# A cached decode block on one core: VectorE's part written as a loop, a head group's output steps placed in the next group's scores, load buffers at multiples of 512 bytes

## The chip, the cores and the metric

The kernel runs on one core of a Trainium2 chip. The core has five engines that work at the same time, each on its own list of instructions: TensorE (PE; its weight loads are listed as PEld), VectorE (DVE), ScalarE (ACT), GpSimd (POOL) and SyncE (SP), which here issues nearly all loads. The loads themselves are carried out by 16 DMA engines. Engines wait for each other through semaphores. The metric is the device time of one execution in microseconds (us); lower is better.

## The reference

One token for each of two sequences goes through grouped-query attention over a cache of 32768 keys and values and, beside it, through a small two-layer network; the two results are multiplied and added to the input. Everything is bf16.

```python
B, Sq, D = 2, 1, 512
Hq, Hkv, Sk, Dh = 32, 8, 32768, 128          # k_cache, v_cache: (B, Hkv, Sk, Dh)
xn = layernorm(A_x)
q = (xn @ wq) as (B, Hq, 1, Dh)              # four query heads share one cache head
scores = einsum("bhqd,bhkd->bhqk", q, k) * Dh ** -0.5
o = einsum("bhqk,bhkd->bhqd", softmax(scores), v)
s = o.reshape(B, Sq, Hq * Dh) @ wo           # wo: (4096, 512)
h2 = gelu(layernorm(xn) @ w3) @ w4           # with S = 1 the shifted branch through w1, w2 gives zero
g = silu(xn + h2)
return A_x + s * g
```

The two caches are 268 MB of the 280.5 MB that are read. Each of their bytes is used once, for four query heads.

## The kernel before

**Tiling.** The 16 pairs of a sequence and a cache head are the head groups (`groups`, L171). A group has 8 MB of keys and 8 MB of values. A group's rows are laid over 128 partitions, 64 KB to each, and its 32768 keys are cut into two halves of 128 keys a partition (`NPART` = 2, `SLOT` = 32 KB a partition). Keys go to `kbuf`, which has three slots of a half; a group uses slots 0 and 1 or 1 and 2 by turns. Values go to `vbuf`, two slots, reused by every group.

**One group, in order.** VectorE transposes the keys of a half in eight steps into four small buffers `T0` to `T3` (L383), 16 steps a group. TensorE multiplies each by the query (L432, four matmuls a step) and sums the eight steps of a half in one PSUM bank, `sc[0]` or `sc[1]`. VectorE takes the largest score of each half (`peak`, L373 and L374), TensorE spreads it (L438), VectorE makes the shift (L390, L391), ScalarE the exponentials (L392), VectorE their transposes (L397). TensorE sums the weights (L443) and multiplies them by the values (L451, 64 matmuls into `o`). Then come the group's **output steps**: ScalarE copies `o` to `ob` (L402); TensorE turns it (`oT`, L460); VectorE divides by the sum (`on`, L403 and L404); TensorE spreads the result (`xp`, L466); VectorE keeps the right quarter of it and stores it in the group's column of `oX` (L405, L408). After the last group TensorE multiplies `oX` by `wo` (L479, 128 small matmuls, 16 for each cache head); VectorE multiplies by `g4` and adds the input (L412, L413); two small stores write the output (L415).

**What sets the order.** Every engine's list is written out by hand. `Queue.op` (L47) puts the wait for the last event it needs on the instruction itself. TensorE's part of the 16 groups is a loop of 16 turns (`nc.Fori`, L423) that counts semaphores down (`take`, L419); VectorE's, ScalarE's and SyncE's parts are written out for all 16 groups. In each engine's list the output steps of a group stand between its values and the next group's keys: VectorE starts the transposes of group m+1 only after L408 of group m.

**The loads.** SyncE issues them in the order wq, w3, w4, keys of group 0, values of group 0, keys of 1, values of 1 and so on, each key or value load as one transfer of 8 MB. The keys of group m wait until the first half of the scores of group m-1 is done (`half`, L334: that frees slot 1, the only slot that two groups in a row share). The values of group m wait until the values of group m-1 have been multiplied (L346). The last group's keys and values come as two transfers each, a half at a time (L342, L330). Behind them, three transfers bring `wo` into slot 0 of `kbuf` (L348: four, three and one of the eight cache heads). L474 makes the products of cache head k wait for its own column of `oX` and its own part of `wo`.

**Where the buffers lie.** The tiles are placed one behind another in the order of L114 to L161, `kbuf` first.

Of the kernel before, what the change touches and what calls it, by code (L numbers as in the profile page):

```python
# [13 lines left out]
PE = mybir.EngineType.PE  # L14

KPT = 128
RT = 16
VT = 4
# [46 lines left out]
def kernel(  # L65
# [32 lines left out]
    SLOT = KPT * Dh  # L98
    NQ = 4
# [8 lines left out]
    def sb(name, shape, dt):  # L108
        return pool.tile(shape, dt, name=name)
# [3 lines left out]

    kbuf = sb("kbuf", [128, 3 * SLOT], BF16)  # L114
# [45 lines left out]
    g = sb("g", [B, D], F32)  # L160
    oX = sb("oX", [128, Hkv, NQ, B], BF16)  # L161

# [12 lines left out]
    def sem(name):  # L175
        return tc.alloc_semaphore(name)
# [12 lines left out]
    d_k = [sem(f"d_k{i}") for i in range(2)]  # L189
    d_wo = [sem(f"d_wo{i}") for i in range(len(wo_parts))]  # L190
    t_T, t_z, t_mx, t_pt, t_ob, t_on = (sem(f"t_{n}") for n in ("T", "z", "mx", "pt", "ob", "on"))
    t_v = [sem(f"t_v{i}") for i in range(NPART)]
    s_T, s_X = sem("s_T"), sem("s_X")
# [9 lines left out]
    NX = 5  # L203

    def order(m):
        return (1, 0) if m % 2 == 0 else (0, 1)

    with tc.tile_critical(no_gpsimd_drain=True):
# [4 lines left out]
        sp.op(lambda e: e.dma_start(out=kbuf[:, 0:NPART * SLOT], in_=row_view(A_k_cache, *groups[0])), inc=(d_k[0], 16))  # L213
# [119 lines left out]
        for m in range(1, NG):  # L333
            half = (s_T, NT * (m - 1) + NR)  # L334
            base = m % 2
            if m < NG - 1:
                sp.op(lambda e, m=m, base=base: e.dma_start(
                    out=kbuf[:, base * SLOT:(base + NPART) * SLOT], in_=row_view(A_k_cache, *groups[m])),
                    half, e_q, inc=(d_k[0], 16))
            else:  # L340
                for h in range(NPART):
                    sp.op(lambda e, m=m, h=h, base=base: e.dma_start(  # L342
                        out=kbuf[:, (base + h) * SLOT:(base + h + 1) * SLOT],
                        in_=row_view(A_k_cache, *groups[m])[:, h * SLOT:(h + 1) * SLOT]),
                        half, inc=(d_k[h], 16))
            load_v(m, (s_X, NX * (m - 1) + 3))  # L346
        for i, (a, c) in enumerate(wo_parts):
            sp.op(lambda e, a=a, c=c: e.dma_start(out=wo3[:, a:c, :], in_=wos[:, a:c, :]), (s_T, NT * (NG - 1)), inc=(d_wo[i], 16))  # L348


        e_oX = [None] * NG
        for m in range(NG):
            b, k = groups[m]
            first, second = order(m)

            def put_z(b, k):
                for j in range(4):
                    c = (NR - 1) * rep + 32 * j
                    ac.op(lambda v, j=j, c=c: v.copy(  # L359
                        out=z[32 * j:32 * j + 32, :, :, c:c + rep],  # L360
                        in_=qr[32 * j:32 * j + 32, :, :, b, k * rep:(k + 1) * rep]),
                        e_qr, e_z0, inc=(t_z, 1) if j == 3 else False)

            if m == 0:
                put_z(b, k)

            def landed(h):
                if m < NG - 1:
                    return (d_k[0], 16 * (m + 1))
                return (d_k[h], 16 * NG if h == 0 else 16)  # L370

            def peak(i):
                e = ve.op(lambda v: v.tensor_reduce(out=mx[:, i:i + 1], in_=sc[i][:, :], axis=AX.X, op=ALU.max), (s_T, m * NT + (i + 1) * NR))  # L373
                ve.op(lambda v: v.tensor_scalar_mul(out=mxr[:, i, :], in0=row_of[:, :], scalar1=mx[:, i:i + 1]), e,  # L374
                      inc=(t_mx, 1) if i == NPART - 1 else False)

            for i, h in enumerate((first, second)):
                u = m % 2 + h
                kt = kbuf[:, u * SLOT:(u + 1) * SLOT].bitcast(I32)
                for r in range(NR):  # L380
                    n = m * NT + i * NR + r
                    used = (s_T, n - T_BUFS + 1) if n >= T_BUFS else None
                    ve.op(lambda v, n=n, r=r, kt=kt: v.transpose(  # L383
                        out=Ts[n % T_BUFS][:, :].rearrange("p (b t k) -> p t b k", b=NB, t=RT),
                        in_=kt[:, r * W:(r + 1) * W].rearrange("p (t b k) -> p t b k", b=NB, t=RT)),
                        landed(h), used, inc=(t_T, 1))
                    if i == 1 and r == 3:
                        peak(0)
            peak(1)
            e = ve.op(lambda v: v.tensor_reduce(out=top[:, :], in_=S[:, rep:], axis=AX.X, op=ALU.max), (s_X, NX * m + 1))  # L390
            e = ve.op(lambda v: v.tensor_scalar_mul(out=shift[:, :], in0=top[:, :], scalar1=-inv_sqrt_dh), e)  # L391
            e_exp = [ac.op(lambda v, i=i: v.activation(  # L392
                out=ep[i][:, :], in_=sc[i][:, :], func=ACT.Exp, scale=inv_sqrt_dh, bias=shift[:, :], accum_out=rs[i][:, :]),
                e, e_tf if m == 0 else None) for i in range(NPART)]
            for i, h in enumerate((first, second)):
                ve.op(lambda v, i=i: v.tensor_scalar_mul(out=sm[i][:, :], in0=sel_h[:, :], scalar1=rs[i][:, 0:1]), e_exp[i], e_selh, inc=False)  # L396
                ve.op(lambda v, i=i, h=h: v.transpose(  # L397
                    out=pt[h][:, :, :].rearrange("p r (t h) -> p t r h", h=rep),
                    in_=ep[i][:, :].rearrange("p (t r h) -> p t r h", r=NR, h=rep)), inc=(t_pt, 1))
            if m < NG - 1:  # L400
                put_z(*groups[m + 1])
            ac.op(lambda v: v.copy(out=ob[:, :], in_=o[:, :]), (s_X, NX * m + 3), inc=(t_ob, 1))  # L402
            e = ve.op(lambda v: v.reciprocal(out=rec[:, :], in_=S[:, 0:rep]), (s_X, NX * m + 2))  # L403
            ve.op(lambda v: v.tensor_mul(out=on[:, :], in0=oT[:, :], in1=rec[:, :]), e, (s_X, NX * m + 4), inc=(t_on, 1))  # L404
            e = ve.op(lambda v: v.tensor_mul(  # L405
                out=xm[:, :, :], in0=xp_b[:, :].rearrange("p (r h) -> p r h", r=NQ), in1=mask[:, :, :]), (s_X, NX * m + 5))
            with nc.allow_low_precision(reason="three of the four terms are zero, the fourth is bf16"):
                e_oX[m] = ve.op(lambda v: v.tensor_reduce(out=oX[:, k, :, b], in_=xm[:, :, :], axis=AX.X, op=ALU.add), e)  # L408
# [10 lines left out]
        def take(s, n=1):  # L419
            nc.tensor.wait_ge(s, n).then_inc(s, -n)  # L420

        pe.wait(e_o0, e_ones, e_const, e_hf, e_tf)
        with nc.Fori(0, NG, engines=[PE], head_slot={PE: 0}):  # L423
            take(t_z)
            for i in range(NPART):
                for r in range(NR):
                    take(t_T)
# [10 lines left out]
            nc.tensor.matmul(  # L438
                S[:, rep:], lhsT=same_h[:, :], rhs=mxr[:, :, :].rearrange("p i r -> p (i r)"),
                start=True, stop=True).then_inc(s_X, 1)  # L440
            take(t_pt, NPART)
            for i in range(NPART):
                ins = nc.tensor.matmul(S[:, 0:rep], lhsT=ones_f[:, :], rhs=sm[i][:, :], start=(i == 0), stop=(i == NPART - 1))  # L443
            ins.then_inc(s_X, 1)
            for h in range(NPART):
                take(t_v[h], 16)
# [10 lines left out]
            ins.then_inc(s_X, 1)  # L457
            take(t_ob)
            for t in range(VT):
                ins = nc.tensor.matmul(  # L460
                    oT[:, :], lhsT=ob[:, t * Dh:(t + 1) * Dh], rhs=sel_o[:, t, :],
                    start=(t == 0), stop=(t == VT - 1))
            ins.then_inc(s_X, 1)
            take(t_on)
            for r in range(NQ):
                ins = nc.tensor.matmul(  # L466
                    xp_b[:, r * rep:(r + 1) * rep], lhsT=sel_r[:, r, :, :].rearrange("p j w -> p (j w)"), rhs=on[:, :],
                    start=True, stop=True)
            ins.then_inc(s_X, 1)
# [43 lines left out]
```

## Time and profile before

| | |
|---|---|
| median of three runs | 662.71 us (662.61 to 662.96) |
| the profiled execution, its own time | 663.0 us |
| span of the profiled execution, first to last instruction | 661.0 us |
| mean granted TensorE clock | 0.812 of full speed |
| busy share of PE, DVE, ACT | 64%, 56%, 8% |
| read from HBM | 280.50 MB, 424 GB/s over the span |

The profile describes one execution. "Busy" counts the time in which an engine's unit works; an engine can be half idle and still set the end, if something late waits for it. A row of DMA queues gives the packets of a queue, their megabytes, and the time that all its packets took as a share of the span times 16 DMA engines. In the timeline a row holds a start, a duration, the engine, the line of the kernel, what is written and from what, and how many instructions are merged (x64); in brackets stands how long the engine had been idle and what ended that. A "landing" is the time from the issue of a transfer to the completion of all its 16 shares.

### The profile page before, as it was taken

The numbers are of one execution on the slowest core, as the hardware profiler recorded it, in microseconds if no ns is written. First come the engines' busy times: TensorE is split into PE (matmuls) and PEld (weight loads), VectorE is DVE, ScalarE is ACT, GpSimd is POOL, SyncE is SP. The second block draws the span as 40 slices with busy tenths as digits, with TensorE's granted clock in tenths as the row PEclk, the third lists the DMA queues.
The fourth block names the chain that finished last, engine by engine and source line by source line (L and its number), as shares of the span: only waits on it lengthen the run. The fifth ranks groups of instructions, "written<-read, shape, count | busy, mean of one in ns | idle before, by whom it ended". The sixth has DMA issues, their size and how long they took to land. (4 is left out here: it accounts for less than half of the span.)

```text
span 661.0 us, 6555 instructions
## 1 busy us (share of the span) xinstructions
PE 422.7 (64%) x2642; PEld 176.3 (27%) x2674; DVE 373.2 (56%) x526; ACT 50.0 (8%) x152; POOL 1.7 (0%) x10
## 2 busy tenths in 40 slices
PE   2537586665758656485865648576565947656775
PEld 2312233222223322232332213222222322222323
DVE  4248192764819376381936629194672928558481
ACT  1110101010010101001010100101010010101000
POOL 1000000000000000000000000000000000000000
PEclk9959687787968769796877979788696976869798
DMA  8999999999999999999999999999999999999994
GB/s 363 444 430 440 437 444 436 409 437 436 440 440 433 420 428 436 444 440 432 412 436 436 445 436 432 412 440 436 444 436 432 412 437 436 444 432 409 424 413 183
DMA packets 6461, 280.61 MB, mean 425 GB/s; under 512 B 682, under 2 KB 692, under 8 KB 1716
## 3 DMA queue, kind: packets, MB, share of 16 engines
q1 hardware_dynamic: 6408, 280.50, 98.4%
q8 instruction: 4, 0.07, 0.0%
q14 instruction: 5, 0.04, 0.0%
q10 hardware_dynamic: 44, 0.01, 0.0%
HBM read 280.50 MB, written 0.00 MB: 424 GB/s over the span
## 5 line engine op out<-in xcount | busy, mean ns | idle before, releaser
L432 PE MATMUL sc<-T,z 128*128 128x512 bf16 x992 | 275.1, 422 | 133.9 <-PEq L420 127.9
L383 DVE STREAM_TRANSPOSE T<-kbuf 128x1024 int32<-128x1024 int32 x256 | 292.1, 1208 | 76.3 <-DMA kbuf<-in_A_k_cache_dram 76.3
L432 PEld LDWEIGHTS sc<-T,z 128*128 128x128 bf16 x1024 | 97.8, 103 | 304.9 <-issue 227.4
L451 PE MATMUL o<-vbuf,pt 128*16 128x512 bf16 x1024 | 92.8, 542 | 0.0
L404 DVE TENSOR_TENSOR on<-oT,rec 128x4 bf16<-128x4 f32 x16 | 2.6, 162 | 117.8 <-PE oT L460 117.8
L392 ACT ACTIVATE ep<-sc,shift 128x512 bf16<-128x512 f32 x32 | 21.7, 683 | 461.2 <-DVE shift L391 461.2
L451 PEld LDWEIGHTS o<-vbuf,pt 128*16 128x16 bf16 x1024 | 31.0, 119 | 54.0 <-issue 47.4
L443 PE MATMUL S<-sm,ones_f 128*128 128x4 f32 x64 | 14.6, 333 | 48.2 <-PEq L420 48.2
L373 DVE TENSOR_REDUCE mx<-sc 128x1 f32<-128x512 f32 x32 | 21.5, 671 | 20.0 <-PE sc L432 20.0
L443 PEld LDWEIGHTS S<-sm,ones_f 128*128 128x128 f32 x64 | 13.6, 298 | 49.9 <-issue 49.9
L460 PE MATMUL oT<-sel_o,ob 128*128 128x4 f32 x128 | 16.4, 252 | 12.6 <-PEq L420 12.6
L397 DVE STREAM_TRANSPOSE pt<-ep 128x512 bf16<-128x512 bf16 x32 | 22.6, 705 | 0.0
L460 PEld LDWEIGHTS oT<-sel_o,ob 128*128 128x128 f32 x128 | 15.5, 191 | 20.2 <-issue 20.2
L438 PE MATMUL S<-mxr,same_h 128*128 128x64 f32 x32 | 6.5, 285 | 18.4 <-PEq L420 18.4
L402 ACT COPY ob<-o 128x512 f32<-128x512 f32 x16 | 9.4, 586 | 113.7 <-PE o L451 113.7
L396 DVE TENSOR_SCALAR sm<-sel_h,rs 128x4 f32<-128x4 f32 x32 | 6.7, 209 | 13.6 <-ACT ep L392 13.6
L359 ACT COPY z<-qr 32x16 bf16<-32x16 bf16 x64 | 12.6, 197 | 3.9 <-issue 3.3
L403 DVE RECIPROCAL rec<-S 128x4 f32<-128x4 f32 x16 | 2.9, 183 | 17.5 <-PE S L443 17.5
L438 PEld LDWEIGHTS S<-mxr,same_h 128*128 128x128 f32 x32 | 4.8, 188 | 26.2 <-issue 26.2
L390 DVE TENSOR_REDUCE top<-S 128x1 f32<-128x64 f32 x16 | 3.6, 225 | 9.4 <-PE S L438 9.4
L374 DVE TENSOR_SCALAR mxr<-row_of,mx 128x32 f32<-128x32 f32 x32 | 7.7, 242 | 1.1
L466 PE MATMUL xp<-on,sel_r 128*128 128x4 bf16 x64 | 3.8, 164 | 5.5 <-PEq L420 5.5
(70 smaller groups left out, 64.2 us busy)
## 6 DMA issues: line engine op xcount, KB each, us to landing
kbuf<-in_A_k_cache_dram SPq DMA_DIRECT2D x2, 4096.0 KB, 22.7
vbuf<-in_A_v_cache_dram SPq DMA_DIRECT2D x2, 4096.0 KB, 21.7
kbuf<-in_A_wq_dram SPq DMA_DIRECT2D x1, 4096.0 KB, 12.4
vbuf<-in_B_w_dram SPq DMA_DIRECT2D x2, 1792.0 KB, 18.9
kbuf<-in_A_wo_dram SPq DMA_DIRECT2D x1, 2048.0 KB, 31.1
kbuf<-in_A_wo_dram SPq DMA_DIRECT2D x1, 1536.0 KB, 34.3
kbuf<-in_A_wo_dram SPq DMA_DIRECT2D x1, 512.0 KB, 34.9
kbuf<-in_A_k_cache_dram SPq DMA_DIRECT2D x15, 28.1
```

What stands on the lines that cost most here:

```text
L359: ac.op(lambda v, j=j, c=c: v.copy(out=z[32 * j:32 * j + 32, :, :, c:c + rep], in_=qr[32 * j:32 * j + 32, :, :, b, k * rep:(k + 1) * rep]) ...
L373: e = ve.op(lambda v: v.tensor_reduce(out=mx[:, i:i + 1], in_=sc[i][:, :], axis=AX.X, op=ALU.max), (s_T, m * NT + (i + 1) * NR))
L374: ve.op(lambda v: v.tensor_scalar_mul(out=mxr[:, i, :], in0=row_of[:, :], scalar1=mx[:, i:i + 1]), e, inc=(t_mx, 1) if i == NPART - 1 else ...
L383: ve.op(lambda v, n=n, r=r, kt=kt: v.transpose(out=Ts[n % T_BUFS][:, :].rearrange("p (b t k) -> p t b k", b=NB, t=RT), in_=kt[:, r * W:(r ...
L392: e_exp = [ac.op(lambda v, i=i: v.activation(out=ep[i][:, :], in_=sc[i][:, :], func=ACT.Exp, scale=inv_sqrt_dh, bias=shift[:, :], accum_ou ...
L397: ve.op(lambda v, i=i, h=h: v.transpose(out=pt[h][:, :, :].rearrange("p r (t h) -> p t r h", h=rep), in_=ep[i][:, :].rearrange("p (t r h) ...
L402: ac.op(lambda v: v.copy(out=ob[:, :], in_=o[:, :]), (s_X, NX * m + 3), inc=(t_ob, 1))
L432: ins = nc.tensor.matmul(sc[i][:, :], lhsT=z[:, nb, w, zc:zc + 128], rhs=Tb[:, nb, :, w], start=(r == 0 and nb == 0 and w == 0), stop=(r = ...
L438: nc.tensor.matmul(S[:, rep:], lhsT=same_h[:, :], rhs=mxr[:, :, :].rearrange("p i r -> p (i r)"), start=True, stop=True).then_inc(s_X, 1)
L443: ins = nc.tensor.matmul(S[:, 0:rep], lhsT=ones_f[:, :], rhs=sm[i][:, :], start=(i == 0), stop=(i == NPART - 1))
L451: ins = nc.tensor.matmul(o[32 * j:32 * j + VT * rep, :], lhsT=pt[h][:, r, a * VT * rep:(a + 1) * VT * rep], rhs=vt[:, u * VT:(u + 1) * VT, ...
L460: ins = nc.tensor.matmul(oT[:, :], lhsT=ob[:, t * Dh:(t + 1) * Dh], rhs=sel_o[:, t, :], start=(t == 0), stop=(t == VT - 1))
```

## The change

Six things are changed.

1. **VectorE's part of the head groups is a loop** of eight turns with two groups a turn (two, because a group's slots of `kbuf` alternate). The waits are no longer on the instructions: each is an instruction of its own in front of the one that needs it (`take`), which also counts the semaphore down. There are new semaphores for this: `t_used` for a `T` buffer that may be overwritten, `t_k[i]` for the i-th half of the keys that is worked on, `t_top`, `t_S`, `t_e`, `t_d`, `t_oT`, `t_xp`.
2. **The output steps of group m stand in the scores of group m+1.** TensorE turns `ob` between the two halves of the scores (`head_oT`) and spreads `on` after the fourth step of the second half (`head_xp`). VectorE divides after `peak(0)` (`head_on`) and keeps the quarter after the last transpose (`head_out`). The first group does these steps on zeros (`ob` is set to zero at the start); after the loops they are done once more for the last group.
3. **`oX` is written by ScalarE.** In a loop VectorE cannot name the group's column, so it writes to `oXs`, and ScalarE, whose part is still written out, copies that into the column (`keep_oX`), ahead of the next exponentials. All products with `wo` now wait for the last of these copies.
4. **The keys of the next group are issued** when the first matmul of `head_oT` behind the first half of the scores is done (`s_half`) in place of when the first half is done.
5. **`wo` is issued** behind the values of group 14 (`s_pv`), as the last values are, where it waited for the last scores of group 14 before; it stood behind the last values in SyncE's list before, and still does.
6. **An unused tile `lead`** of 384 bytes a partition ahead of `kbuf` puts `kbuf` and `vbuf` at multiples of 512 bytes; the tiles began at byte 16512 of a partition (`SB0`).

```diff
+    SB0 = 16512
+    sb("lead", [128, (-SB0) % 512 // 2], BF16)
     kbuf = sb("kbuf", [128, 3 * SLOT], BF16)
...
+    oXs = sb("oXs", [128, NQ], BF16)
...
+        po.op(lambda e: e.memset(ob[:, :], 0.0), inc=(t_ob, 1))
...
-            half = (s_T, NT * (m - 1) + NR)
...
-                    half, e_q, inc=(d_k[0], 16))
+                    (s_half, m), e_q, inc=(t_k[0], 16))
+                nc.sync.sem_inc(t_k[1], 16)
...
-            load_v(m, (s_X, NX * (m - 1) + 3))
+            load_v(m, (s_pv, m))
...
-            sp.op(lambda e, a=a, c=c: e.dma_start(out=wo3[:, a:c, :], in_=wos[:, a:c, :]), (s_T, NT * (NG - 1)), inc=(d_wo[i], 16))
+            sp.op(lambda e, a=a, c=c: e.dma_start(out=wo3[:, a:c, :], in_=wos[:, a:c, :]), (s_pv, NG - 1), inc=(d_wo[i], 16))
...
+        def keep_oX(m):
+            b, k = groups[m]
+            return ac.op(lambda v: v.copy(out=oX[:, k, :, b], in_=oXs[:, :]), (s_oX, m + 2))
...
         for m in range(NG):
+            if m:
+                keep_oX(m - 1)
+            for i in range(NPART):
+                ac.op(lambda v, i=i: v.activation(
+                    out=ep[i][:, :], in_=sc[i][:, :], func=ACT.Exp, scale=inv_sqrt_dh, bias=shift[:, :], accum_out=rs[i][:, :]),
+                    (s_shift, m + 1), e_tf if m == 0 else None, inc=(t_e, 1))
...
+        e_oX = keep_oX(NG - 1)
...
+        def head_on():
+            take(nc.vector, t_oT, 2)
+            nc.vector.tensor_mul(out=on[:, :], in0=oT[:, :], in1=rec[:, :]).then_inc(t_on, 1)
+
+        def head_out():
+            take(nc.vector, t_xp)
+            nc.vector.tensor_mul(
+                out=xm[:, :, :], in0=xp_b[:, :].rearrange("p (r h) -> p r h", r=NQ), in1=mask[:, :, :]).then_inc(t_d, 1)
+            take(nc.vector, t_d)
             with nc.allow_low_precision(reason="three of the four terms are zero, the fourth is bf16"):
-                e_oX[m] = ve.op(lambda v: v.tensor_reduce(out=oX[:, k, :, b], in_=xm[:, :, :], axis=AX.X, op=ALU.add), e)
+                nc.vector.tensor_reduce(out=oXs[:, :], in_=xm[:, :, :], axis=AX.X, op=ALU.add).then_inc(s_oX, 1)
+
+        def take(eng, s, n=1):
+            eng.wait_ge(s, n).then_inc(s, -n)
...
+        ve.op(lambda v: v.memset(rec[:, :], 1.0), inc=(t_oT, 1))
+        with nc.Fori(0, NG // 2, engines=[DVE], head_slot={DVE: 0}):
+            for par in range(2):
+                for i, h in enumerate(order(par)):
+                    take(nc.vector, t_k[i], 16)
+                    u = par + h
+                    kt = kbuf[:, u * SLOT:(u + 1) * SLOT].bitcast(I32)
+                    for r in range(NR):
+                        n = i * NR + r
+                        if n >= T_BUFS:
+                            take(nc.vector, t_used)
+                        nc.vector.transpose(
+                            out=Ts[n % T_BUFS][:, :].rearrange("p (b t k) -> p t b k", b=NB, t=RT),
+                            in_=kt[:, r * W:(r + 1) * W].rearrange("p (t b k) -> p t b k", b=NB, t=RT)).then_inc(t_T, 1)
+                        if i == 1 and r == 3:
+                            peak(0)
+                            head_on()
+                head_out()
+                take(nc.vector, t_used, T_BUFS)
+                peak(1)
...
+                take(nc.vector, t_S)
+                nc.vector.reciprocal(out=rec[:, :], in_=S[:, 0:rep]).then_inc(t_oT, 1)
+        head_on()
+        head_out()
...
-                    ins.then_inc(s_T, 1)
-            take(t_mx)
+                    ins.then_inc(t_used, 1)
+                    if i == 1 and r == 3:
+                        head_xp()
+                if i == 0:
+                    head_oT(s_half)
+            take(nc.tensor, t_mx)
...
-            ins.then_inc(s_X, 1)
-            take(t_ob)
-            for t in range(VT):
-                ins = nc.tensor.matmul(
-                    oT[:, :], lhsT=ob[:, t * Dh:(t + 1) * Dh], rhs=sel_o[:, t, :],
-                    start=(t == 0), stop=(t == VT - 1))
-            ins.then_inc(s_X, 1)
-            take(t_on)
...
+            ins.then_inc(s_pv, 1)
+        head_oT()
+        head_xp()
...
-                pe.wait(e_s0, e_oX[(B - 1) * Hkv + k], (d_wo[i], 16))
+                pe.wait(e_s0, e_oX, (d_wo[i], 16))
```

`head_oT` and `head_xp` hold the same matmuls as L460 and L466, four each; with the argument `s_half`, `head_oT` raises that semaphore behind its first matmul.

More of the change, by code (lines that the diff above doesn't have):

```diff
@@ L14 @@
 PE = mybir.EngineType.PE
+DVE = mybir.EngineType.DVE
 KPT = 128
@@ L344 @@
                         in_=row_view(A_k_cache, *groups[m])[:, h * SLOT:(h + 1) * SLOT]),
-                        half, inc=(d_k[h], 16))
-            load_v(m, (s_X, NX * (m - 1) + 3))
+                        (s_half, m), inc=(t_k[i], 16))
+            load_v(m, (s_pv, m))
         for i, (a, c) in enumerate(wo_parts):
-            sp.op(lambda e, a=a, c=c: e.dma_start(out=wo3[:, a:c, :], in_=wos[:, a:c, :]), (s_T, NT * (NG - 1)), inc=(d_wo[i], 16))
-        e_oX = [None] * NG
-        for m in range(NG):
[L353 to L399, printed above, removed]
@@ new lines, with put_z @@
+            sp.op(lambda e, a=a, c=c: e.dma_start(out=wo3[:, a:c, :], in_=wos[:, a:c, :]), (s_pv, NG - 1), inc=(d_wo[i], 16))
+        def put_z(b, k):
+            for j in range(4):
+                c = (NR - 1) * rep + 32 * j
+                ac.op(lambda v, j=j, c=c: v.copy(
+                    out=z[32 * j:32 * j + 32, :, :, c:c + rep],
+                    in_=qr[32 * j:32 * j + 32, :, :, b, k * rep:(k + 1) * rep]),
+                    e_qr, e_z0, inc=(t_z, 1) if j == 3 else False)
+        def keep_oX(m):
+            b, k = groups[m]
+            return ac.op(lambda v: v.copy(out=oX[:, k, :, b], in_=oXs[:, :]), (s_oX, m + 2))
@@ L400 @@
+        put_z(*groups[0])
+        for m in range(NG):
+            if m:
[4 more added lines that the diff above has]
+                    (s_shift, m + 1), e_tf if m == 0 else None, inc=(t_e, 1))
             if m < NG - 1:
                 put_z(*groups[m + 1])
-            ac.op(lambda v: v.copy(out=ob[:, :], in_=o[:, :]), (s_X, NX * m + 3), inc=(t_ob, 1))
@@ L416, with head_oT, head_xp @@
         sp.wait((d_out, 32))
-        def take(s, n=1):
-            nc.tensor.wait_ge(s, n).then_inc(s, -n)
+        def head_oT(first=None):
+            take(nc.tensor, t_ob)
+            for t in range(VT):
+                ins = nc.tensor.matmul(
+                    oT[:, :], lhsT=ob[:, t * Dh:(t + 1) * Dh], rhs=sel_o[:, t, :],
+                    start=(t == 0), stop=(t == VT - 1))
+                if t == 0 and first is not None:
+                    ins.then_inc(first, 1)
+            ins.then_inc(t_oT, 1)
+        def head_xp():
+            take(nc.tensor, t_on)
+            for r in range(NQ):
+                ins = nc.tensor.matmul(
+                    xp_b[:, r * rep:(r + 1) * rep], lhsT=sel_r[:, r, :, :].rearrange("p j w -> p (j w)"), rhs=on[:, :],
+                    start=True, stop=True)
+            ins.then_inc(t_xp, 1)
         pe.wait(e_o0, e_ones, e_const, e_hf, e_tf)
         with nc.Fori(0, NG, engines=[PE], head_slot={PE: 0}):
-            take(t_z)
+            take(nc.tensor, t_z)
             for i in range(NPART):
                 for r in range(NR):
-                    take(t_T)
+                    take(nc.tensor, t_T)
                     Tb = Ts[(i * NR + r) % T_BUFS][:, :].bitcast(BF16).rearrange("p (b c e) -> p b c e", b=NB, e=2)
```

46 lines of the change are left out of this document (28 added, 18 removed).

## The prediction

> **What bounds the kernel now.** I read the page's span and queue rows first, since a kernel that reads 280 MB may be bound by its loads.
>
> ```profile
> span 661.0 us, 6555 instructions
> ...
> PE 422.7 (64%) x2642; PEld 176.3 (27%) x2674; DVE 373.2 (56%) x526; ACT 50.0 (8%) x152; POOL 1.7 (0%) x10
> ...
> q1 hardware_dynamic: 6408, 280.50, 98.4%
> q8 instruction: 4, 0.07, 0.0%
> q14 instruction: 5, 0.04, 0.0%
> ```
>
> The load queue's packets fill 98.4% of the time of 16 DMA engines. The few "instruction" packets are code being fetched; they matter below. Next the table of stretches (span, busy time of PE, PEld, DVE, ACT, POOL, granted clock, DMA share, GB/s), one stretch from the middle and four from the end:
>
> ```profile
> 100.00:200.00 100.00, 61.51 (x379) 25.42 (x383) 51.58 (x76) 8.14 (x27) 0.00 (x0) 0.78 1.00 434
> ...
> 651.00:652.00 1.00, 1.00 (x24) 0.48 (x20) 0.00 (x0) 0.00 (x0) 0.00 (x0) 0.99 0.56 229
> 652.00:653.00 1.00, 0.47 (x12) 0.00 (x0) 0.00 (x0) 0.47 (x1) 0.00 (x0) 1.00 0.14 57
> 653.00:654.00 1.00, 0.74 (x7) 0.77 (x7) 0.00 (x0) 0.11 (x1) 0.00 (x0) 1.00 0.06 25
> 654.00:655.00 1.00, 0.53 (x7) 0.39 (x7) 0.26 (x2) 0.00 (x0) 0.00 (x0) 1.00 0.04 16
> ```
>
> In the middle the share is 1.00 at 434 GB/s: the loads never pause. At the end the share falls to 0.06, a sixteenth: **one DMA engine alone** is still loading. The queue row of the stretch 652.6 to 656 says for how long:
>
> ```profile
> q1 hardware_dynamic: 15, 0.05, 3.8%
> ```
>
> 3.8% of 16 x 3.4 us is 2.07 us. A transfer has landed only when its slowest share has, so this engine, 2.1 us behind the rest, sets every landing. Now the SyncE issues from the timeline:
>
> ```profile
> 307.24 0.33 SPq L325 DMA_DIRECT2D vbuf<-in_A_v_cache_dram  x1
> 324.90 0.33 SPq L337 DMA_DIRECT2D kbuf<-in_A_k_cache_dram  x1
> 345.38 0.33 SPq L325 DMA_DIRECT2D vbuf<-in_A_v_cache_dram  x1
> 363.06 0.33 SPq L337 DMA_DIRECT2D kbuf<-in_A_k_cache_dram  x1
> ...
> 403.34 0.33 SPq L337 DMA_DIRECT2D kbuf<-in_A_k_cache_dram  x1
> ...
> 597.89 0.80 SPq L342 DMA_DIRECT2D kbuf<-in_A_k_cache_dram  x2
> ...
> 619.22 8.19 SPq L348 DMA_DIRECT2D kbuf<-in_A_wo_dram  x3
> ```
>
> And landings, in us behind the issue: the key loads issued at 324.90, 363.06 and 403.34, with the instruction queue of the stretch 363 to 367; then the halves of the last keys (min/median/max), and the last part of `wo`.
>
> ```profile
> kbuf<-in_A_k_cache_dram SPq DMA_DIRECT2D x1, 27.7
> ...
> kbuf<-in_A_k_cache_dram SPq DMA_DIRECT2D x1, 29.3
> ...
> kbuf<-in_A_k_cache_dram SPq DMA_DIRECT2D x1, 27.7
> ...
> q14 instruction: 1, 0.01, 0.5%
> ...
> DMA to landing us min/median/max: 18.0/22.7/27.4
> ...
> kbuf<-in_A_wo_dram SPq DMA_DIRECT2D x1, 512.0 KB, 34.9
> ```
>
> The keys land at 352.6, 392.4 and 431.0: steps of 39.8 and 38.7. At 434 GB/s 16.78 MB take 38.7, so the first step has 1.0 us too much, and in that stretch one 8 KB packet of code was fetched. So **a code fetch costs the engine it falls on about 1.0 us**, and its delay stays to the end.
>
> Last, the end itself: the timeline where group 14 gives way to group 15, then the chain of waits.
>
> ```profile
> 619.11 1.03 PE L460 MATMUL oT<-sel_o,ob 128*128 128x4 f32 x8 [0.79 <-PEq L420]
> ...
> 620.97 0.17 DVE L408 TENSOR_REDUCE oX<-xm 128x4 bf16<-128x16 f32 x1
> 621.05 13.62 DVE L383 STREAM_TRANSPOSE T<-kbuf 128x1024 int32<-128x1024 int32 x12
> ```
>
> ```profile
> 654.63 0.24 PE xp L466 x4
> 654.87 0.14 issue
> 655.01 1.99 PE pro L479 x128
> 657.00 0.02 issue
> 657.02 0.30 DVE sg L412
> ```
>
> `wo` lands at about 655.1 (the last of three issues, some 1.0 us into its row, plus 34.9), and the products with `wo` start at 655.01 because the last group's output steps end only then. So **two things end together**: the loads, and the calculation of the last two groups. The first half of the last keys lands at 615.9 (597.89 + 18.0), but its transposes start at 621.05, behind the output steps of group 14: 5.1 us are lost there.
>
> **The change part by part.** The sum is made against the start of `sg`, 657.02; from there to the end of the span 4.0 us stay as they are.
>
> *Output steps moved.* The transposes of the last group can start with the landing at 615.9, and the second half's with the landing of the second keys, near 625.7 (issued by 598.3, plus 27.4), where they start at 630.1 now (621.05 + 8 x 13.62/12): 4.4 us earlier. Against this the group gets the matmuls of L460 (1.03), those of L466 (0.24) and VectorE's `on`, some 0.3 with its hop. TensorE can hide much of its part, as VectorE fills four buffers ahead; I count 1.0 in all, between 0.3 and 1.6. The chain up to `xp` then ends 3.4 us earlier, at 651.5. Behind it come now L408 (0.17 by its row), L405, of no more elements, and their hops, 0.4 together, and ScalarE's copy with its hops, 0.4 by the small copies of the row below. Before, the first 112 products ran over L405 and L408, since they needed only earlier columns.
>
> ```profile
> L359 ACT COPY z<-qr 32x16 bf16<-32x16 bf16 x64 | 12.6, 197 | 3.9 <-issue 3.3
> L383 DVE STREAM_TRANSPOSE T<-kbuf 128x1024 int32<-128x1024 int32 x256 | 292.1, 1208 | 76.3 <-DMA kbuf<-in_A_k_cache_dram 76.3
> ```
>
> So the products can start at 652.3, and the 112 of the first seven cache heads (1.99 x 112/128 = 1.74) end at 654.0, before `wo` lands at 655.1. Only the last 16 (0.25) stand behind the landing: `sg` at 655.4. **This part gives 1.6 us**, and from here the loads set the end. In the 15 groups before, the moved steps cost nothing: VectorE waits 76.3/15 = 5.1 us a group for keys, and that covers them.
>
> *VectorE's loop.* Written out, its list is fetched as code all along, and three of the five q14 packets fall after 180 us:
>
> ```profile
> q14 instruction: 3, 0.02, 0.0%
> ```
>
> With 526 instructions, about 30 a group, VectorE is the only engine with that much new code then (TensorE loops, ScalarE has 152 in all). A loop that stays in the engine's memory drops these three. They cost 3 x 1.0 us on one engine, but that engine is only 2.1 us behind the next one (the share of 0.06), so landings come **2.1 us** earlier. Ends: 0, if the packets are not VectorE's, and 2.1. I take 2.1. The extra waits, 25 a group, run while a transpose does; their price is nothing to 0.2 us each before they would use up the 5.1 us, and I take nothing. The loop's entry has the time until the first keys are there, 42.8 us:
>
> ```profile
> L383 DVE STREAM_TRANSPOSE T<-kbuf x256: 1200/1203/1246, 42.8 to 638.9; 128x1024 int32<-128x1024 int32 x128
> ```
>
> *Copies of `oX`, the moved triggers.* The copies stand on ScalarE ahead of exponentials that come 10 us later: nothing. The key load is issued one small matmul later, at most 1 us. A key load is issued (324.90) while the values before it are still landing (issued at 307.24, some 26 us), and the next values (345.38) 7.2 us before the keys land at 352.6, so no queue runs dry: nothing. `wo` stands behind the last values as before: nothing.
>
> *Buffers at multiples of 512 bytes.* No row has both kinds. What alignment can save is at most the part of a packet's time that does not grow with its size. The lone engine's last stretch gives it: 13 packets of 4 KB (two of the 15 are tiny) in 2.07 us are 0.159 us each; at the stream's 434/16 = 27.1 GB/s 4 KB take 0.151. So 8 ns a packet are fixed. An engine has 6408/16 = 400 packets, some 360 of them with data: 2.9 us. Ends 0 and 2.9 (no row speaks for a loss); I take the middle, **1.4**.
>
> [...]
>
> *Sum.* `wo` lands at 655.1 - 2.1 - 1.4 = 651.6. The chain in front of the products moves with the key landings, so its 654.0 becomes about 651; `sg` starts at 651.6 + 0.3 = 651.9, 5.1 us before 657.02. The profiled execution's own time is 663.0 (the median of the runs is 662.7, 0.3 lower): 657.9 there, **657.6 us** for the runs.
>
> **The rivals.**
>
> *Only the moved steps pay* (the q14 packets remain, alignment does nothing): 662.7 - 1.6 = 661.1. For it: no row names the packets' engine. Against it: no other engine has the code.
>
> *The loop fetches its code anew.* Place: the jump back of each of the eight turns; price 1.0 us on one DMA engine for each 8 KB packet. Eight fetches in place of three set that engine back by 5 us: with alignment's 1.4, `wo` lands at 658.7, `sg` is at 659.0, and the run takes 664.7. It is slower from six fetches on, since 655.1 - 1.4 + 3 + 0.3 = 657.0 is where `sg` was. With two blocks a turn it is 16 fetches and 672.7. Against it: TensorE loops 16 times already, with a longer body, and q8 has four packets in all. For it: VectorE's body is 30 instructions and some 25 waits a group, 110 a turn. Three packets served the 12 groups after 180 us, 30 instructions each, so a packet is an estimated 120 instructions: a turn nearly fills one.
>
> [...]
>
> *The calculation stays last.* If each of the 25 waits adds 0.1 us, the last two groups lose 5 us: the products start at 652.3 + 5, less the 3.3 by which the keys land earlier, at 654.0, all of `wo` is there, and 128 products (1.99) put `sg` at 656.0. That is 661.7, close to no change; at 0.15 us each it is 664.2.
>
> *The loads starve.* Waits over 0.2 us each take more than the 5.1 us of cover; at 0.3 it is 2.4 us a group, 38 in all: 700.
>
> **How the numbers follow.** The forecast has 0.65, the moved steps alone 0.13, the loop's fetches 0.10, the calculation last 0.09, starved loads 0.03. The forecast's own range is 656.1 (alignment worth 2.9) to 659.5 (alignment nothing, half a us of delay in the chain). The first rival carries the range on to 661.3. Below I go to 654.5, because the other 15 engines do not end together either (shares of 0.56 and 0.14 over 1.5 us), and if code fetches spread them as well, that goes too. What a measurement can tell from no change is 0.2%, 1.3 us: 661.4 to 664.0. Faster: 0.65, 0.10 of the first rival and 0.04 of the third, 0.79; same: 0.03 and 0.05, 0.08; slower: 0.10 + 0.03 = 0.13.
>
> **What would show it.** Right: the products with `wo` in two pieces, the last 16 behind the landing; `sg` near 652; the last group's transposes beginning with the landing of its first half; at most two or three q14 packets, none after 180 us; the DMA share ending within about 0.5 us where it now trails at 0.06 for 2.1; 435 GB/s in the middle. Wrong: q14 packets in every turn; 434 GB/s as before (alignment worth nothing); a middle share under 1.00, or transposes that take over 1.14 us a step.

## The result, and the profile after

Six runs of the changed kernel have a median of 659.62 us (659.08 to 660.24); six runs of the kernel before 662.78 us (662.14 to 664.77). The ratio is 0.9943, with a 95% interval of 0.9926 to 0.9961: the change makes the kernel about 0.6% faster; the medians lie 3.2 us apart. The profiled execution took 659.97 us. The runs of a kernel fall into groups: three of the changed kernel took 659.08 to 659.27 and three, the profiled one among them, 659.97 to 660.24, and the kernel before, with its runs of the later rounds, took either 661.4 to 663.1 or 664.0 to 665.5.

Page of the changed kernel, span and queues, and below them the instruction queue of the stretch from 180 us to the end:

```profile
span 657.6 us, 7019 instructions
...
q1 hardware_dynamic: 6408, 280.50, 98.7%
q8 instruction: 4, 0.07, 0.0%
q14 instruction: 4, 0.03, 0.0%
```

```profile
q14 instruction: 1, 0.01, 0.0%
```

Three q14 packets fell after 180 us before; now there is one, and the trace has it at 657.0, when all loads are over. The table of stretches, the stream first, then the end (span, busy time of PE, PEld, DVE, ACT, POOL, granted clock, DMA share, GB/s):

```profile
120.00:580.00 460.00, 297.66 (x1728) 126.17 (x1752) 269.35 (x360) 34.95 (x120) 0.00 (x0) 0.81 1.00 435
...
648.00:649.00 1.00, 0.50 (x7) 0.35 (x6) 0.16 (x1) 0.00 (x0) 0.00 (x0) 1.00 1.01 414
649.00:650.00 1.00, 0.07 (x6) 0.10 (x10) 0.34 (x2) 0.20 (x1) 0.00 (x0) 0.51 0.61 250
650.00:651.00 1.00, 1.00 (x44) 1.00 (x47) 0.00 (x0) 0.00 (x0) 0.00 (x0) 0.50 0.19 78
651.00:652.00 1.00, 1.00 (x48) 1.00 (x40) 0.00 (x0) 0.00 (x0) 0.00 (x0) 0.50 0.02 8
652.00:653.00 1.00, 1.00 (x60) 0.87 (x48) 0.00 (x0) 0.00 (x0) 0.00 (x0) 0.79 0.05 16
```

The loads still never pause (share 1.00). They end near 651.3 (0.02 of 16 engines is 0.3 us of one), where one engine went on to about 654.6 before (0.04 in the microsecond from 654). But the granted clock of TensorE falls to 0.50 at 649.0 (the mean of that microsecond is 0.51) and is back at 1.00 at 652.4; in the kernel before it was 1.00 over its last microseconds.

Timeline of the last group, landings of the two halves of the last keys (min/median/max) and of the last part of `wo`, and the chain of waits:

```profile
612.81 9.24 DVE L416 STREAM_TRANSPOSE T<-kbuf 128x1024 int32<-128x1024 int32 x8 [1.91 <-DVEq L396]
616.44 7.16 PE L477 MATMUL sc<-T,z 128*128 128x512 bf16 x31 [0.17 <-PEq L396]
617.17 7.12 SPq L354 DMA_DIRECT2D kbuf<-in_A_wo_dram  x3
622.62 4.62 DVE L416 STREAM_TRANSPOSE T<-kbuf 128x1024 int32<-128x1024 int32 x4 [0.57 <-DVEq L396]
640.15 6.30 PE L500 MATMUL o<-vbuf,pt 128*16 128x512 bf16 x64
649.64 0.20 ACT L367 COPY oX<-oXs 128x4 bf16<-128x4 bf16 x1 [2.54 <-DVE oXs L393]
653.12 0.29 DVE L442 TENSOR_TENSOR sg<-pro,g 98x128 f32<-98x128 f32 x1 [3.51 <-PE pro L518]
653.76 0.67 SPq L445 DMA_DIRECT2D out_dram<-out  x1
```

```profile
DMA to landing us min/median/max: 17.2/21.9/26.5
...
kbuf<-in_A_wo_dram SPq DMA_DIRECT2D x1, 512.0 KB, 33.5
```

```profile
648.72 0.24 PE xp L462 x4
648.96 0.97 issue
649.93 3.16 PE pro L518 x126
653.09 0.02 issue
653.12 0.30 DVE sg L442
```

Three things are to be seen. The transposes of the last group start at 612.81, with the landing of the first half, and the second half's at 622.62, with its own landing. `wo` lands at about 651.7 (617.17 + 1.0 + 33.5), 3.4 us earlier than before. And the products with `wo` start at 649.93, after TensorE has stood idle for 0.97 us waiting for the copies of `oX`, and take 3.16 us where they took 1.99: the chain that ends last is the calculation, 1.4 us behind the landing.

### The profile page after: what moved, and what is told of

The parts are those of the page before. It is cut to its first block, busy times and chain, and to the rows that moved or that the text cites. A ratio compares the mean times of both kernels' runs of the same rounds, so it can differ in the third digit from the quotient of the medians.

```text
span 657.6 us, 7019 instructions
## 1 busy us (share of the span) xinstructions
PE 413.3 (63%) x2654; PEld 180.6 (27%) x2686; DVE 372.4 (57%) x530; ACT 53.1 (8%) x168; POOL 2.2 (0%) x11
## 5 line engine op out<-in xcount | busy, mean ns | idle before, releaser
L416 DVE STREAM_TRANSPOSE T<-kbuf 128x1024 int32<-128x1024 int32 x256 | 292.8, 1210 | 177.4 <-DVEq L396 177.4
L477 PE MATMUL sc<-T,z 128*128 128x512 bf16 x992 | 270.8, 420 | 146.7 <-PEq L396 142.5
L477 PEld LDWEIGHTS sc<-T,z 128*128 128x128 bf16 x1024 | 99.7, 104 | 304.4 <-issue 221.4
L500 PE MATMUL o<-vbuf,pt 128*16 128x512 bf16 x1024 | 91.1, 535 | 0.0
L367 ACT COPY oX<-oXs 128x4 bf16<-128x4 bf16 x16 | 3.1, 196 | 375.8 <-DVE oXs L393 375.8
L452 PEld LDWEIGHTS oT<-sel_o,ob 128*128 128x128 f32 x136 | 17.7, 191 | 4.0 <-issue 1.3
## 6 DMA issues: line engine op xcount, KB each, us to landing
kbuf<-in_A_wo_dram SPq DMA_DIRECT2D x1, 512.0 KB, 33.5
```

The costliest lines, as they stand in the source:

```text
L416: nc.vector.transpose(out=Ts[n % T_BUFS][:, :].rearrange("p (b t k) -> p t b k", b=NB, t=RT), in_=kt[:, r * W:(r + 1) * W].rearrange("p (t ...
L452: ins = nc.tensor.matmul(oT[:, :], lhsT=ob[:, t * Dh:(t + 1) * Dh], rhs=sel_o[:, t, :], start=(t == 0), stop=(t == VT - 1))
L477: ins = nc.tensor.matmul(sc[i][:, :], lhsT=z[:, nb, w, zc:zc + 128], rhs=Tb[:, nb, :, w], start=(r == 0 and nb == 0 and w == 0), stop=(r = ...
L500: ins = nc.tensor.matmul(o[32 * j:32 * j + VT * rep, :], lhsT=pt[h][:, r, a * VT * rep:(a + 1) * VT * rep], rhs=vt[:, u * VT:(u + 1) * VT, ...
```

## The experiments

| kernel | median us (runs) | ratio to before, interval | `wo` lands |
|---|---|---|---|
| changed kernel | 659.62 (6) | 0.9943, 0.9926 to 0.9961 | 651.7 |
| a1, before with aligned buffers | 662.19 (12) | 0.9987, 0.9970 to 1.0004 | 652.8 |
| a2, changed, not aligned | 661.17 (12) | 0.9964, 0.9949 to 0.9979 | 652.8 |
| a3, changed, turns written out | 664.16 (12) | 1.0013, 0.9998 to 1.0028 | 656.7 |
| a4, changed, each product waits for its column | 659.30 (6) | 0.9938, 0.9915 to 0.9960 | 651.6 |
| a5, changed, TensorE kept busy | 658.90 (6) | 0.9927, 0.9907 to 0.9947 | 651.5 |
| a7, changed, output steps back in their group | 662.98 (12) | 0.9992, 0.9978 to 1.0006 | 651.8 |
| a8, a4 with idle matmuls before the second part of `wo` | 659.03 (6) | 0.9929, 0.9909 to 0.9949 | 651.8 |
| a9, a4 and a5 together | 659.08 (6) | 0.9929, 0.9907 to 0.9950 | 651.6 |
| 224 bytes beyond a multiple of 256 | 661.12 (10) | 0.9962, 0.9947 to 0.9977 | 653.5 |
| 256 bytes, not 512 | 660.05 (5) | 0.9935, 0.9910 to 0.9960 | 651.6 |
| 32 bytes beyond a multiple of 256 | 661.47 (10) | 0.9964, 0.9949 to 0.9980 | 653.4 |

The last column is worked out as above, from the issue row, 1.0 us and the landing of the last part. Each ratio is taken to the runs of the kernel before that stood beside that kernel. Their median was 662.91 beside a1 to a4, 663.02 beside a5, a7, a8 and the 224 bytes, 664.42 beside a9 and the other two, on three chips. The changed kernel itself was not run again beside these, so a few tenths of a microsecond between it and one of them can be a difference of rounds.

### a1: aligned buffers alone

```diff
--- before
+    sb("lead", [128, (-16512) % 512 // 2], BF16)
     kbuf = sb("kbuf", [128, 3 * SLOT], BF16)
```

> The kernel before with the unused tile alone (buffers at multiples of 512 bytes, nothing else). Theory: alignment saves about 4 ns of each 64 KB packet, because eight of them and their semaphore write took 19.35 us before and 19.32 after; that is about 1.0 us over the stream, so wo lands near 654 in place of 655.1, the last keys land 0.9 earlier, the calculation follows them, and the run takes 661.8. Rival 1, alignment does nothing: 662.8. Rival 2, alignment is the whole gain: 659.6.

Measured: 662.19, between the theory's 661.8 and no change, and the interval holds 1. The twelve runs lie in two groups, six from 660.06 to 661.29 and six from 663.09 to 663.84, so the median of all says little here. The 29 runs of the kernel before beside them lie in two groups as well, 16 from 661.45 to 663.05 and 13 from 664.10 to 665.48. Group against group, a1 is 1.3 us faster in both (medians 661.0 against 662.3, 663.6 against 664.9), near the 1.0 of the theory. What makes the groups was not tried. Alignment is not the whole gain.

### a2: the changed kernel without alignment

```diff
--- changed
-    sb("lead", [128, (-SB0) % 512 // 2], BF16)
```

> The changed kernel without the unused tile (buffers at byte 16512 again). Theory: every landing from the middle on is later, by 1.0 us at the end, the calculation with it: 660.6. Rival 1, alignment does nothing: 659.6. Rival 2, alignment is the whole gain: 662.8.

Measured: 661.17; by the medians alignment is worth 1.55 us in the changed kernel, and `wo` lands 1.1 later without it. Rows of this kernel, the chain of waits:

```profile
649.46 0.24 PE xp L461 x4
649.70 0.97 issue
650.67 3.61 PE pro L517 x127
```

The chain is 0.7 later at `xp`, and the products are slower by another 0.45: 3.61 us is what they took at a granted clock of 0.50 throughout in the kernel 224 bytes beyond a multiple of 256 (below), where the changed kernel had 1.00 again from 652.4 on. That 0.45 comes from the clock and not from the loads.

### a3: VectorE's turns written out

```diff
--- changed
-        with nc.Fori(0, NG // 2, engines=[DVE], head_slot={DVE: 0}):
+        for turn in range(NG // 2):
```

> The changed kernel with VectorE's eight turns written out, the same instructions in the same order. Theory: its 880 instructions are fetched in about seven packets of 8 KB on one DMA engine, about 1.0 us each; that engine is up to 0.8 us ahead of the slowest at first, so wo lands some 5 to 6 us later, near 657, and the run takes 664 to 665, slower than before. Rival, code fetches do not matter (they fit into gaps of the stream, or the landings are not what sets the end): 659.6, with landings as in the changed kernel.

Measured: 664.16, as the theory had it. Instruction packets of this kernel on the page, its stretches at the end, and the issue of `wo` with its last landing:

```profile
q8 instruction: 4, 0.07, 0.0%
q14 instruction: 9, 0.07, 0.0%
```

```profile
654.00:655.00 1.00, 0.81 (x60) 0.84 (x64) 0.00 (x0) 0.09 (x1) 0.00 (x0) 1.00 0.07 29
655.00:656.00 1.00, 0.74 (x52) 0.55 (x42) 0.00 (x0) 0.00 (x0) 0.00 (x0) 0.91 0.06 25
656.00:657.00 1.00, 0.99 (x40) 0.71 (x34) 0.00 (x0) 0.00 (x0) 0.00 (x0) 0.50 0.08 25
```

```profile
620.89 8.43 SPq L354 DMA_DIRECT2D kbuf<-in_A_wo_dram  x3
```

```profile
kbuf<-in_A_wo_dram SPq DMA_DIRECT2D x1, 512.0 KB, 34.8
```

With the same instructions, q14 has nine packets in place of four, about one engine's share is loading at the end again (0.06 to 0.08), and `wo` lands 5.0 us later. So the added packets are VectorE's code, and what the loop saves is fetching them. Five more packets and 5.0 us agree with the 1.0 us that one was priced at; that the engine was a little ahead of the slowest at first is within that. The 5.0 us is not what the loop gains against the kernel before: that kernel's list had its waits on the instructions and was shorter, with five packets in all.

### a4: each product waits for its own column of `oX`

```diff
--- changed
-                keep_oX(m - 1)
+                e_oX[m - 1] = keep_oX(m - 1)
...
-                pe.wait(e_s0, e_oX, (d_wo[i], 16))
+                pe.wait(e_s0, e_oX[(B - 1) * Hkv + k], (d_wo[i], 16))
```

> The changed kernel with one part undone: the products with wo wait for the copy of their own column of oX again, not all for the last. Theory (the calculation sets the end, not the landing of wo at 651.7): the products start at 649.1 right behind xp, not at 649.93, and TensorE has no idle stretch of 1.0 us; at half clock they take 3.1 us and sg starts at 652.3, 658.8; at full clock the last 16 wait for wo and sg starts at 652.1, 658.6. Rival, the landing of wo or the end behind sg sets the time: 659.6 as in the changed kernel.

Measured: 659.30, 0.3 under the changed kernel where 0.8 to 1.0 was expected. Timeline of this kernel:

```profile
647.95 1.06 PE L519 MATMUL pro<-kbuf,oX 128*2 128x128 bf16 x64
650.49 1.83 PE L519 MATMUL pro<-kbuf,oX 128*2 128x128 bf16 x64 [1.47 <-DMA kbuf<-in_A_wo_dram]
652.37 0.29 DVE L443 TENSOR_TENSOR sg<-pro,g 98x128 f32<-98x128 f32 x1 [3.71 <-PE pro L519]
```

The first 64 products run at once, at 1.06 us. Then TensorE waits 1.47 us for the *second* part of `wo`, which lands only some 1.2 us before the last. The clock falls again, at 650.6, and the second 64 take 1.83. I had counted 112 products as free of the late landings; the 48 of the second part wait as well, and only 64 are free.

### a5: TensorE kept busy in the changed kernel

Nine matmuls whose result nobody reads are put into the waits behind the last group.

```diff
--- changed
+        def busy(n):
+            for _ in range(n):
+                nc.tensor.matmul(
+                    qrb[:, :], lhsT=ident[:, :], rhs=Ts[0][:, 0:256].bitcast(BF16), start=True, stop=True)
+
+        busy(3)
         head_oT()
+        busy(2)
         head_xp()
+        busy(4)
```

> The changed kernel with nine idle matmuls (128x512, into an unused bank) in TensorE's waits behind the last group: three before oT, two before xp, four before the products with wo. Theory: the products took 3.13 us because the granted clock fell to 0.50 in TensorE's wait of 0.97 us for the copies of oX; kept busy, the clock stays at 1.00 there, the products take about 2.0 and sg starts 0.8 to 1.0 us earlier: 658.7. Rival 1, the products are slow for another reason (late parts of wo, their operands): they take 3.1 at a clock of 1.00, 659.6. Rival 2, the idle matmuls delay the chain by what they take: above 659.6.

Measured: 658.90, 0.7 below the changed kernel. The stretches and the timeline of this kernel:

```profile
650.00:651.00 1.00, 1.00 (x76) 1.00 (x80) 0.00 (x0) 0.00 (x0) 0.00 (x0) 1.00 0.23 94
651.00:652.00 1.00, 1.00 (x68) 0.72 (x56) 0.00 (x0) 0.00 (x0) 0.00 (x0) 1.00 0.07 20
```

```profile
649.97 2.04 PE L526 MATMUL pro<-kbuf,oX 128*2 128x128 bf16 x128
652.07 0.29 DVE L442 TENSOR_TENSOR sg<-pro,g 98x128 f32<-98x128 f32 x1 [2.43 <-PE pro L526]
```

The products start at the same time as in the changed kernel (649.97 and 649.93) and take 2.04 us at a clock of 1.00, where they took 3.16 at 0.50. So with the waits filled the clock stayed at 1.00, and that is worth 1.1 us in this pair of profiles. In the times it is less sure: a5's six runs (658.79 to 659.21) lie 0.2 below the faster three of the changed kernel and 1.2 below the slower three. No trace of the faster three was kept, so whether their products ran at full clock is not shown.

The theory's cause, the wait of 0.97 us ahead of the products, does not hold. In the kernel with its buffers at 256 bytes (below), whose last steps are the same instructions, TensorE's matmuls of `xp` start at 648.25, the wait at 648.50 and the products at 649.47. Its stretches (granted clock third from the end):

```profile
648.00:648.25 0.25, 0.00 (x0) 0.03 (x1) 0.10 (x1) 0.00 (x0) 0.00 (x0) 0.69 1.03 426
648.25:648.50 0.25, 0.25 (x4) 0.16 (x4) 0.00 (x0) 0.00 (x0) 0.00 (x0) 0.50 0.94 377
648.50:649.47 0.97, 0.00 (x1) 0.03 (x1) 0.34 (x2) 0.20 (x1) 0.00 (x0) 0.50 1.04 427
```

The clock was down already while `xp` ran, before that wait began; in the changed kernel it fell 0.06 us into it. And a7, below, has the same wait of 0.97 us, and its products take 1.96 us at a clock of 1.00. So what the fall followed lies further back, among the waits of 0.79 us ahead of `oT` and 0.46 us ahead of `xp`, which a5 fills too. They are not the whole cause either: a7 has these two waits as well, and its clock stayed at 1.00. TensorE was busy for 2.1 of the 3.4 us before the fall in the changed kernel, for 3.4 of the same stretch in a5, and for 2.2 of the 3.4 us up to `xp` in a7. The granted clock changed at 645.6, 649.0 and 652.4 in the changed kernel and at 644.2 and 651.0 in the kernel before, 3.4 and 6.8 us apart, so it may count how the waits lie to these times. That is a guess of mine and was not tried; what sets the clock is not shown.

### a7: the output steps back at the end of their group

```diff
--- changed
                         if i == 1 and r == 3:
                             peak(0)
-                            head_on()
-                head_out()
...
                 nc.vector.reciprocal(out=rec[:, :], in_=S[:, 0:rep]).then_inc(t_oT, 1)
-        head_on()
-        head_out()
+                head_on()
+                head_out()
...
                     ins.then_inc(t_used, 1)
-                    if i == 1 and r == 3:
-                        head_xp()
                 if i == 0:
-                    head_oT(s_half)
+                    nc.tensor.sem_inc(s_half, 1)
...
             ins.then_inc(s_pv, 1)
-        head_oT()
-        head_xp()
+            head_oT()
+            head_xp()
```

> The changed kernel with the output steps at the end of their own group again (loops, copies of oX, triggers and aligned buffers kept; the first group's empty steps go). Theory: landings as in the changed kernel (wo at 651.7), but the last group's transposes start some 5 us later, behind the output steps of group 14, near 618, and the products start near 653.5: 661.5 to 663. Rival, the stream alone sets the end and the move is worth nothing: 659.6.

ScalarE's copy of `oX` stands behind its own group's `ob` again too, and the first group's output steps on zeros, with their two memsets, are left out.

Measured: 662.98, the upper end of the theory and the median of the kernel before (663.02 in these runs, between its two groups). The timeline of this kernel:

```profile
619.25 0.17 DVE L390 TENSOR_REDUCE oXs<-xm 128x4 bf16<-128x16 f32 x1
619.39 13.64 DVE L412 STREAM_TRANSPOSE T<-kbuf 128x1024 int32<-128x1024 int32 x12
...
654.49 1.96 PE L510 MATMUL pro<-kbuf,oX 128*2 128x128 bf16 x128 [0.97 <-ACT oX L366]
```

`wo` lands at 651.8, 3.3 us earlier than before, and the median gains nothing from it: the last group's transposes wait for the output steps of group 14 until 619.39, 6.6 us later than in the changed kernel, and the products start at 654.49. Part of that is the price of the copies of `oX`, which a7 keeps: TensorE waits 0.97 us ahead of the products, and 0.14 in the kernel before.

### a8 and a9: keeping the clock in a4

a8 puts six of a5's unread matmuls in front of the wait for the second part of `wo` in a4; a9 puts five there, three before `oT` and two before `xp`.

> The kernel in which each product with wo waits for its own column of oX, with six idle matmuls between the fourth cache head's products and the wait for the second part of wo. There the products stood still for 1.5 us, the clock fell to 0.50, and the last 64 took 1.83 us. Theory: with the clock kept at 1.00 these 64 take 1.0 us, or end with the last part's landing plus 0.3, at 652.0 in place of 652.35: 658.8 to 659.0, about 0.5 below 659.3. Rival, the landing of the last part sets it in both: 659.3.

> Both mends of the end together: each product with wo waits for its own column of oX, and idle matmuls keep TensorE busy before oT, before xp and before the wait for the second part of wo. Theory: with the clock kept at 1.00 the landing of the last part of wo (651.7) is now what ends last, as it nearly was with idle matmuls alone, so this gives sg at 652.0 and 658.8, no more than 0.1 below 658.9. Rival, the calculation still sets the end: sg before 651.7 cannot be, so a gain of 0.5 or more would show that the landing is earlier than I take it to be.

Measured: 659.03 and 659.08, neither apart from a5. In the profiled run of a8 (661.1 us; its other five took 658.84 to 659.40) the clock had fallen to 0.50 at 649.4, before the unread matmuls came, and these then took 2.49 us and delayed the products, so it decides nothing about its theory. It shows a fall that no wait of 1 us preceded, only those of 0.79 and 0.46 us. The profiled run of a9:

```profile
648.72 1.06 PE L528 MATMUL pro<-kbuf,oX 128*2 128x128 bf16 x64
649.94 1.03 PE L510 MATMUL qrb<-T,ident 128*128 128x512 bf16 x4 [0.16 <-issue]
650.90 1.23 PE L528 MATMUL pro<-kbuf,oX 128*2 128x128 bf16 x64
652.18 0.29 DVE L443 TENSOR_TENSOR sg<-pro,g 98x128 f32<-98x128 f32 x1 [2.75 <-PE pro L528]
```

Both mends hold and `sg` is still at 652.18, as in a5 (652.07): from here the landing of `wo` at 651.6 sets the end. a9 fills the waits ahead of `oT` and `xp` alone in front of its first 64 products, and these took 1.06 us, as in a4 at a granted clock of 1.00. By the medians the two mends give 0.5 to 0.7 us against the changed kernel.

### Where the buffers begin

Three kernels change only the size of the unused tile, `(off - SB0) % 512` bytes with `off` 224, 256 and 32.

> The changed kernel with its buffers at 224 bytes beyond a multiple of 256, in place of 0 (and of 128 before). Theory, the time grows with the distance beyond a multiple of 256 bytes: at 128 a 64 KB packet lost about 4 ns, at 224 it loses about 7, so the stream ends some 1.7 us later than aligned, and the run takes 661.3 to 661.5. Rival, any start that is not aligned costs the same as 128: 661.2 with landings as without the unused tile.

> The changed kernel with its buffers at an odd multiple of 256 bytes, so at 256 but not at 512. Theory, a multiple of 256 is enough: landings as aligned to 512 (the last packet of wo ends near 651.3), 659.6. Rival, 512 is needed: landings as at 128 and at 224 (652.4 to 653.1), 661.1.

> The changed kernel with its buffers at 32 bytes beyond a multiple of 256. Theory 1, a start that is not a multiple of 256 costs a packet some 4 ns whatever the distance (as 128 did, 4.0, and 224 nearly, 4.9): 661.0. Theory 2, the cost grows with the distance, from 0 at 0 to 4 at 128: at 32 it is 1 ns, and the run takes 659.9.

The times of the packets in the trace give a finer measure than the run: the median time in which one DMA engine does eight packets of 64 KB and the semaphore write behind them.

| start beyond a multiple of 256 bytes | eight packets, us | more for a packet, ns | median us |
|---|---|---|---|
| 0 (multiple of 512) | 19.319 | 0 | 659.62 |
| 0 (odd multiple of 256) | 19.319 | 0 | 660.05 |
| 32 | 19.359 | 5.0 | 661.47 |
| 128 | 19.352 | 4.1 | 661.17 |
| 224 | 19.358 | 4.9 | 661.12 |

Here a multiple of 256 did as well as one of 512: 19.319 us in both. The products of the last four rows took 3.61 us in the profiled runs (with 224 bytes at a granted clock of 0.50 from first to last), so the 1.1 to 1.4 us between 660.05 and the rows below it are not the clock's. At 32, 128 and 224 bytes beyond a multiple of 256 a packet took 5.0, 4.1 and 4.9 ns more: the theory of a cost that grows with the distance, which I held at 224, is wrong at 32.

## Why the prediction was right

**The landing of `wo`**: forecast 651.6, measured 651.7, 3.4 us earlier than before. *Alignment* has 1.1 of it by a2 (1.5 in the time); the 1.4 that was forecast was the middle between 0 and 2.9, so that it came so near is luck. For *VectorE's loop* 2.3 are left, where 2.1 were forecast: no q14 packet falls between 180 us and the end of the loads, and a3 shows that such packets are VectorE's, at about 1.0 us each.

**Output steps moved**: the last group's transposes start with the landings, as forecast. The price of 1.6 us, with the landings standing still, was not measured: no run has the move alone. Taken out of the changed kernel (a7), the move costs 3.4 us (662.98 - 659.62), because with the landings earlier the calculation is what ends last. The parts do not add: to undo one costs 4.5 in a3, 3.4 in a7 and 1.55 in a2, where the whole change is 3.2.

**Costed at nothing, and it was**: the extra waits (a transpose takes 1210 ns on the mean, 1208 before) and the moved triggers (share 1.00 in the stream, 435 GB/s as forecast). The loop's fetches, the slower transposes and the starved loads, three of the rivals, did not come; nor did the first, as q14's packets went. The calculation does end last, as one rival had it, but not through slower waits.

**What was wrong** is the end, by 2.0 us (659.6 against 657.6). The measured time lies just above the forecast's own range (656.1 to 659.5) and inside the wider one only, which a rival that did not come had carried on to 661.3. "From here the loads set the end" did not hold: the products did not fall into two pieces with the last 16 behind the landing, and `sg` came at 653.12, not 651.9. The products began at 649.93, 0.9 later than the 649.0 that follows from the forecast's 652.3: `xp` ended at 648.96, 0.8 later, and the wait behind it was 0.97 in place of 0.8. They took 3.16 us in place of 1.99: the row of before showed them at a clock of 1.00, and I took their duration over into a place where the clock was 0.50. a5 shows that this is the clock. The second slip is "from there to the end of the span 4.0 us stay as they are": it was 4.5. The store's issue to the end of the span took 3.8 us (653.76 to 657.6) and 3.3 before (657.67 to 661.0); why was not tried. The last 0.3 lie outside the span (659.97 - 657.6 = 2.4, before 2.0).

## What to carry to other kernels

Where loads and calculation end together, look at both ends before pricing an edit: in a7 a landing 3.3 us earlier left the median where it was, since the calculation could not follow. In the kernel before one DMA engine went on alone for 2.07 us, to about 654.6, and `wo` landed at about 655.1, so look for an engine that trails at the end, and for what it carries beside the loads, such as code (a3: five more packets of code, `wo` 5.0 us later, one engine's share left at the end). Before a duration is taken over into another place, check that the granted clock there is the same, and look for the moment at which it changed before naming the wait that did it.

## What the runs showed of the hardware that was not expected

- Among the short, dependent matmuls of the last steps the granted clock of TensorE fell from 1.00 to 0.50, with no wait over 0.8 us ahead of the fall (256 bytes: down before the longest wait began). In the changed kernel the 128 small products then took 3.16 us, and 2.04 with the waits filled. In a7, with the same waits, it stayed at 1.00.
- With five more 8 KB packets of VectorE's code fetched, `wo` landed 5.0 us later in a3, about 1.0 us for each, and the stream had not made that up by its end.
- Loads into buffers at 32, 128 and 224 bytes beyond a multiple of 256 took 5.0, 4.1 and 4.9 ns more for each 64 KB packet than at a multiple of 256 or 512.
